# Second attention by whole units of 384 tokens, and a float32 path with TensorE transposes for two batches and two units

## The chip, the cores and the metric

The kernel runs on one core of a Trainium2 chip, written in Bass with the Tile framework. The metric is the time of one execution on the device, in microseconds; lower is better. The core's engines are TensorE (PE in the profile, its weight loads PEld), VectorE (DVE), ScalarE (ACT), GpSimd (POOL) and SyncE (SP). Each runs its own queue of instructions in order. All of this kernel's transfers, transposes by DMA included, are issued from SP's queue.

## The reference

The inputs are q, k, v of shape [8, 8, 576, 64] (batch, head, token, dimension), p of shape [8, 8, 32, 64], and the weights of a gated feed-forward layer, which arrive as 64-bit floats.

```python
def sm_attn(qq, kk, vv):
    s = scale * np.matmul(qq, kk.transpose(0, 1, 3, 2))      # scale = 1/8
    s = s - np.max(s, axis=-1, keepdims=True)
    a = np.exp(s)
    a = a / (np.sum(a, axis=-1, keepdims=True) + 1e-09)
    return np.matmul(a, vv)
p_packed = sm_attn(p, k, v)              # first attention: 32 rows per head
out = sm_attn(q, p_packed, p_packed)     # second attention: 576 tokens over 32 keys
# x: [4608, 512], a token's 8 heads side by side
xn = x / np.sqrt(np.mean(x * x, axis=-1, keepdims=True) + 1e-06) * rms_g
g = xn @ w_gate                          # [512, 1536]
val = xn @ w_val
return (g * (1 / (1 + np.exp(-g))) * val @ w_out)   # w_out [1536, 512]
```

## The kernel before

A product of float32 matrices is made of three f16 matmuls: each operand is scaled and split into a high and a low half (`split`: ACT makes the high half at L127, DVE the low one at L128), and high·high, high·low and low·high are added up in PSUM. Beside f16 there is a float32 path, which needs no split.

The 4608 tokens make 12 units of 384 tokens (`UT`), a unit is 3 tiles of 128 tokens. A batch has 576 tokens, one and a half units, so units 1, 4, 7 and 10 hold tokens of two batches ("mixed" below).

First attention, by batch: `stage1_gen(b)`. It loads the keys (`kf`, L254) and p, takes norms (Square with output `khl`, L390), splits the keys and transposes them by DMA (`kT`, L311), scores `psc` on PE (L331), softmax, transposes of the probabilities on PE (`pat`, L354), values `pp`. Batch 0 instead stays in float32, with keys transposed by TensorE (L295) and scores at L322. Its end result, p_packed, is folded into the gate and value weights: `pw_chunk(b, c)` makes six chunks per batch (`pp_w` on PE at L463, then four ACT and four DVE splits into `pwt`), two of them during the unit ahead and four in the first unit that needs them.

Second attention, by tile of 128 tokens: `qtile_gen(t)` loads q (`qf`, L500), takes its norm and splits it (`qhl`), transposes it by DMA (`qT`, L525), makes the scores `ps` on PE (L550; float32 at L541 for the tiles of unit 0), then max, subtract (L557), exp (ACT, L558), sum, reciprocal and product on DVE, splits the probabilities (`ehl`), transposes them by DMA (`aT`, L574), multiplies by the values (`px`, L581; ACT squares it at L587 for the RMS norm) and POOL makes the norm (`ru`, L594). `unit_gen(u)` then joins the three tiles: a sum over the unit on PE (`pnu`, L609), the scale `rr` by tile, a second split (`ahl`) and a third DMA transpose by tile (`aTu`, L633). Unit 0 has TensorE transposes in place of all three (`pqT` at L505, and `transposed`).

The feed-forward of a unit has two phases. In the first, called gv here, `moe_ft` runs for 12 slices of 128 features: PE makes `pg` and `pv` (L659), ACT applies silu (`t`, L666), DVE multiplies (L667), ACT and DVE split the product into `h` (L669, L670). `pg`, `pv`, `po` and `pp_w` share four PSUM buffers. In the second, called out here, `moe_out` runs 36 matmuls `po` (L680) for each of 3 tiles, DVE scales the result and SP stores it.

The order comes from two places. Python generators are stepped in a written order: a string `PROLOGUE` for the start, then 24 slots per unit, one after each `moe_ft` and one after each group of `po` matmuls; `spread` puts the steps of a generator at slots. The framework's scheduler then orders each engine's queue from that, by its own estimates, and places the semaphores. The step `w` of the prologue is the weight load `weights_gen`, which includes w_out (`wst` loads, conversion to float32, `wo_split` into `wo` at L224 to L229). `big` is a rotating set of buffers (5 in this kernel) for `kf`, `vf`, `khl`, `kT` and the first q.

Where the second attention stands among the slots:

```python
    for t in range(TPU, NU * TPU):
        u, i = divmod(t, TPU)
        at = NS * (u - 1) + 4 * i + 2
        spread(qtile_gen(t), [at - 6, at, at + 3, at + 7, at + 8])
    for u in range(1, NU):
        at = NS * (u - 1) + 19
        spread(unit_gen(u), [at, at + 1, at + 2, at + 3, at + 4])
```

Of the kernel before, what the change touches and what calls it, by code (L numbers as in the profile page):

```python
# [28 lines left out]
def tile_packed_attention_then_swiglu(  # L29
# [41 lines left out]
    HR = H * NPK  # L71
    QK = 1.0 / math.sqrt(D)
# [75 lines left out]
    wctx = ExitStack()  # L148
    wpool = wctx.enter_context(tc.tile_pool(name="wpool", bufs=2))
# [11 lines left out]
    def load_gv(c):  # L161

        pn = ps_m.tile([P, 512], F32, name="pn", tag="pm")
        for n, w in enumerate((w_gate, w_val)):

            room = (2 * c + n) % 5
            if room < 3:
                raw = wo32[:, 4 * room : 4 * room + 4, :].bitcast(U32).rearrange("p a n -> p (a n)")
            else:
                raw = wpool.tile([P, 4 * DM], U32, name="wst", tag="wst", bufs=2)  # L170
# [24 lines left out]
    def load_wo(i):  # L195

        raw = wpool.tile([P, 2, DM, 2], U32, name="wst", tag="wst", bufs=2)
# [4 lines left out]
        to_f32(wo32[:, 2 * i : 2 * i + 2, :], raw)  # L202
        nc.vector.tensor_reduce(
            wo_mx[:, 2 * i : 2 * i + 2], wo32[:, 2 * i : 2 * i + 2, :], AX.X, ALU.max, apply_absolute_value=True
        )

    def wo_scale():

        v = wo_mx.rearrange("p (c f) -> p c f", f=2)
        nc.vector.tensor_mul(v, v, wo_sc.unsqueeze(2).broadcast_to([P, NFC, 2]))  # L210
        mx = wpool.tile([P, 1], F32, name="wmx", tag="w1", bufs=6)
        nc.vector.tensor_reduce(mx, wo_mx, AX.X, ALU.max)
# [18 lines left out]
    def weights_gen():  # L231
        load_g()
        yield
# [3 lines left out]
        for i in range(NFT // 2):  # L237
            load_wo(i)
            yield
        wo_scale()  # L240
        for i in range(NFT // 2):
            wo_split(i)
            yield
# [15 lines left out]
    def stage1_gen(b):  # L259
# [5 lines left out]
        if b == 0:  # L265
# [48 lines left out]
        def scores(g, kT):  # L314
# [3 lines left out]
            if b == 0:  # L318
# [43 lines left out]
        def values(vf, a1T, ri, ss):  # L362

            pp = ps_a.tile([P, 512], F32, name="pp", tag="pa")
            for c in range(NCK):
                for j in range(4):

                    cv = c if b else 2 * (c % HC) + c // HC
# [12 lines left out]
        if b == 0:  # L381
# [41 lines left out]
        if b == 0:  # L423
            first_p.append(pool.tile([P, 4, 2, NPK], F32, name="pbd32", tag="pwt", bufs=8))
            nc.gpsimd.memset(first_p[0], 0.0)
# [6 lines left out]
        for g in range(2):  # L432
            h = slice(64 * g, 64 * g + 64)
            if b == 0:
                nc.vector.tensor_copy(first_p[0][h, :, g, :], pts[h])
            nc.scalar.copy(pbd[h, 0, :, g, :], pts[h])
            nc.vector.tensor_tensor(pbd[h, 1, :, g, :], pts[h], pbd[h, 0, :, g, :], ALU.subtract)
# [36 lines left out]
    first_q = []  # L474
    aTs, e32s, rus, units = {}, {}, {}, {}

    late = []

    def qtile_gen(t):
        u, i = divmod(t, TPU)  # L480

        def mem(name, shape, dt, tag, bufs):

            if t < TPU:
                return pool.tile(shape, dt, name=name, tag="pwt", bufs=8)
            return late[0].tile(shape, dt, name=name, tag=tag, bufs=bufs)

        b0, r0 = divmod(t * P, S)
        parts = [(b0, r0, 0, min(P, S - r0))]
        if r0 + P > S:  # L490
            parts.append((b0 + 1, 0, S - r0, P - (S - r0)))
        if t < TPU:
            if t == 0:
                first_q.append(big([P, TPU, H, D], F32, "q0"))
                nc.sync.dma_start(first_q[0], q[0, :, :UT, :].rearrange("h (s c) d -> s c h d", c=TPU))
            qf = first_q[0][:, t, :, :]
        else:
            qf = mem("qf", [P, H, D], F32, "qf", 2)
# [3 lines left out]
        if t < TPU:  # L502
            ps = ps_m.tile([P, 512], F32, name="pqT", tag="pm")
            for kt in range(NKT):
                nc.tensor.transpose(ps[:, kt * P : (kt + 1) * P], qf[:, 2 * kt : 2 * kt + 2, :].rearrange("s h d -> s (h d)"), ident32)  # L505
            qT = mem("qT32", [P, NKT, P], F32, "", 0)
            nc.vector.tensor_copy(qT.rearrange("p k t -> p (k t)"), ps)
            uq = None
        else:
            uq, qT = split_q(qf, mem)  # L510
        yield
        yield from rest_q(t, u, i, parts, qT, uq, mem)

    def split_q(qf, mem):
        qm = pool.tile([P, 1], F32, name="qm", tag="t1", bufs=14)
        uq = pool.tile([P, 1], F32, name="uq", tag="uq", bufs=6)
        sq = pool.tile([P, 1], F32, name="sq_", tag="t1", bufs=14)
        qhl = mem("qhl", [P, 2, H * D], F16, "qhl", 2)
        nc.scalar.activation(
            qhl[:, 0, :].bitcast(BF16).rearrange("s (h d) -> s h d", h=H), qf, AF.Square, accum_out=qm  # L520
        )
        norm_scale(uq, sq, qm)
        split(*(qhl[:, l, :].rearrange("s (h d) -> s h d", h=H) for l in range(2)), qf, sq)
        qT = mem("qT", [P, 2 * NKT, P], F16, "qT", 2)
        nc.sync.dma_start_transpose(out=qT, in_=qhl.rearrange("s l x -> s (l x)"))  # L525
        return uq, qT

    def rest_q(t, u, i, parts, qT, uq, mem):
        b0 = parts[0][0]
        esc = pool.tile([P, 1], F32, name="esc", tag="uq", bufs=6)  # L530
        eps = packs[b0][1]
        if len(parts) > 1:
            eps = pool.tile([P, 1], F32, name="eps2", tag="eps2", bufs=2)
        ps2 = ps_a.tile([P, H, NPK], F32, name="ps2", tag="pa")
        ps2p = ps2.rearrange("s (e j) r -> s e j r", e=2)
        for b, r, o, n in parts:
            uv, eb, _, pbd, _ = packs[b]
            if uq is None:
                nc.vector.tensor_scalar_mul(esc, uv, 0.5 * QK)
                for pi in range(4):  # L540
                    nc.tensor.matmul(  # L541
                        ps2p[:, :, pi, :], qT[:, pi, :], first_p[0][:, pi, :, :], start=True, stop=True
                    )
                continue
            nc.vector.tensor_scalar(esc[o : o + n], uq[o : o + n], uv[o : o + n], 0.25 * QK, ALU.mult, ALU.mult)
            if len(parts) > 1:
                nc.gpsimd.tensor_copy(eps[o : o + n], eb[o : o + n])
            for pi in range(4):
                for j, (lq, lp) in enumerate(((0, 0), (0, 1), (1, 0))):
                    nc.tensor.matmul(  # L550
                        ps2p[o : o + n, :, pi, :], qT[:, lq * NKT + pi, o : o + n], pbd[:, lp, pi, :, :],
                        start=(j == 0), stop=(j == 2),
                    )
        mx = pool.tile([P, H], F32, name="mx2", tag="t8", bufs=6)
        nc.vector.tensor_reduce(mx, ps2, AX.X, ALU.max)  # L555
        e = pool.tile([P, H, NPK], F32, name="e", tag="e", bufs=4)
        nc.vector.tensor_tensor(e, ps2, mx.unsqueeze(2).broadcast_to([P, H, NPK]), ALU.subtract)  # L557
        nc.scalar.activation(e, e, AF.Exp, scale=esc)  # L558
        sm = pool.tile([P, H], F32, name="sm2", tag="t8", bufs=6)
        nc.vector.tensor_reduce(sm, e, AX.X, ALU.add)  # L560
        ri = pool.tile([P, H], F32, name="ri2", tag="t8", bufs=6)
        nc.vector.tensor_scalar(ri, sm, 1e-9, None, ALU.add)
        nc.vector.reciprocal(ri, ri)
        nc.vector.tensor_tensor(e, e, ri.unsqueeze(2).broadcast_to([P, H, NPK]), ALU.mult)
        ef = e.rearrange("s h r -> s (h r)")
        e32s[t] = ef
        aT = mem("aT", [P, 4, P], F16, "aT", 1)
        if t < TPU:
            transposed(aT[:, :2, :], aT[:, 2:, :], ef, 2.0**14)
        else:  # L570
            ehl = mem("ehl", [P, 2, HR], F16, "ehl", 3)
# [232 lines left out]
```

## Time and profile before

| What | Value |
|---|---|
| runs | 901.73, 900.35, 901.82 us, median 901.73 |
| the profiled execution: its time, its span | 899.14 us, 897.3 us |
| mean granted TensorE clock | 0.949 |
| stages: first `pg` of unit 0, first `po` of unit 0 | 80.2 us, 134.3 us |
| first `pg` of units 1 to 6 | 193.8, 264.8, 326.3, 393.4, 461.4, 524.1 us |
| first `pg` of units 7 to 11 | 592.3, 659.1, 721.6, 787.2, 846.6 us |

The span is the part of an execution that the profiler's engine records cover; the execution's time is 1.84 us more. A unit starts at its first gate matmul. Up to 193.8 us the core loads weights, runs the first attention of batch 0 and unit 0; from there to 846.6 us ten units follow one another, each with the attention of later ones in between; the last unit has nothing beside it. In the profile's groups an "idle before" is idle time of that engine just ahead of the group's instructions, with what ended it.

### The profile page before, as it was taken

The numbers are of one execution on the slowest core, as the hardware profiler recorded it, in microseconds if no ns is written. First come the engines' busy times: TensorE is split into PE (matmuls) and PEld (weight loads), VectorE is DVE, ScalarE is ACT, GpSimd is POOL, SyncE is SP. The second block draws the span as 40 slices with busy tenths as digits, with TensorE's granted clock in tenths as the row PEclk, the third lists the DMA queues.
The fourth block names the chain that finished last, engine by engine and source line by source line (L and its number), as shares of the span: only waits on it lengthen the run. The fifth ranks groups of instructions, "written<-read, shape, count | busy, mean of one in ns | idle before, by whom it ended". The sixth has DMA issues, their size and how long they took to land.

```text
span 897.3 us, 16663 instructions
## 1 busy us (share of the span) xinstructions
PE 762.6 (85%) x6392; PEld 433.7 (48%) x6392; DVE 543.7 (61%) x1397; ACT 554.7 (62%) x1065; POOL 85.9 (10%) x219
## 2 busy tenths in 40 slices
PE   4656758748989898999899889999899899989998
PEld 3432324336645444557455435458455345467453
DVE  3686964636737558467557558368466568466351
ACT  3476676436757569567568479467477578476240
POOL 1243005100000000100010100000000100100000
PEclk8567998959999999999999999999999999999999
DMA  9784263430671472230841652231822712220200
GB/s 246 274 302 139 95 140 75 104 70 7 125 156 30 91 166 54 48 89 7 176 105 31 127 129 54 48 89 31 182 72 60 144 34 56 58 60 19 59 1 36
DMA packets 174000, 84.98 MB, mean 95 GB/s; under 512 B 149216, under 2 KB 161504, under 8 KB 173920
## 3 DMA queue, kind: packets, MB, share of 16 engines
q1 hardware_dynamic: 173920, 83.91, 39.5%
q8 instruction: 50, 0.82, 0.4%
q14 instruction: 30, 0.25, 0.1%
HBM read 47.97 MB, written 9.44 MB: 64 GB/s over the span
## 4 chain that ended last, share of the span: by engine, by line
PE 41%; ACT 20%; DVE 16%; DMA 13%; issue 7%; POOL 2%; SPq 1%; ACTq 0%; DVEq 0%; POOLq 0%
PE po L680 13%; PE pg L659 8%; PE pv L659 8%; DMA aT<-ehl 6%; PE pp_w L463 4%; ACT t L666 3%; ACT L666 3%; PE px L581 2%; DMA kT<-khl 2%; DVE t L667 2%; DMA kf<-in_k_dram 2%; ACT pwt L127 2%; DVE pwt L128 1%; DMA aTu<-ahl 1%; ACT khl L390 1%
## 5 line engine op out<-in xcount | busy, mean ns | idle before, releaser
L680 PE MATMUL po<-wo,h 128*128 128x512 f16 x1296 | 295.1, 382 | 3.8 <-ACT t L666 1.4
L659 PEld LDWEIGHTS <-pwt 128*128 128x128 f16 x2304 | 206.0, 99 | 148.2 <-issue 43.5
L659 PE MATMUL pg<-aTu,pwt 128*128 128x384 f16 (+1 forms) x1152 | 170.6, 289 | 38.7 <-ACT t L666 14.1
L680 PEld LDWEIGHTS <-h 128*128 128x128 f16 x1296 | 123.8, 99 | 156.5 <-issue 20.2
L659 PE MATMUL pv<-aTu,pwt 128*128 128x384 f16 (+1 forms) x1152 | 167.9, 289 | 1.3 <-DVE t L667 0.7
L667 DVE SCALAR_TENSOR_TENSOR t<-pv,usc,t 128x384 f32<-128x384 f32 x144 | 88.3, 614 | 51.6 <-PE pv L659 31.6
L128 DVE SCALAR_TENSOR_TENSOR pwt<-pp_w,pw_sc,pwt 128x256 f16<-128x256 f32 x192 | 84.3, 477 | 53.9 <-ACT pwt L127 52.3
L669 ACT CAST h<-t 128x384 f16<-128x384 f32 x144 | 73.0, 509 | 61.2 <-DVE t L667 60.9
L666 ACT ACTIVATE t<-pg,usc 128x384 f32<-128x384 f32 x144 | 83.0, 578 | 35.6 <-PE pg L659 34.4
L127 ACT ACTIVATE pwt<-pp_w,pw_sc 128x256 f16<-128x256 f32 x192 | 81.5, 470 | 21.7 <-PE pp_w L463 12.2
L670 DVE TENSOR_TENSOR h<-t,h 128x384 f16<-128x384 f32 x144 | 79.8, 555 | 21.5 <-ACT h L669 18.7
L587 ACT ACTIVATE px<-px 128x512 f32<-128x512 f32 x36 | 21.0, 584 | 87.6 <-PE px L581 87.4
L463 PE MATMUL pp_w<-wgv,pg 64*32 64x512 f32 x768 | 57.1, 613 | 2.9 <-ACT t L666 2.1
L685 DVE TENSOR_SCALAR o<-po,invE 128x512 f32<-128x512 f32 x36 | 27.0, 749 | 48.6 <-PE po L680 37.0
L581 PE MATMUL px<-pav,aT 128*128 128x256 f16 (+1 forms) x240 | 32.6, 282 | 23.9 <-DMA aT<-ehl 23.4
L589 POOL TENSOR_SCALAR var<-ssx,eps 128x1 f32<-128x1 f32 x36 | 9.5, 265 | 427.2 <-ACT px L587 427.0
L666 ACT ACT_TABLE_LOAD x35 | 44.9, 1283 | 1.5 <-PE pg L659 0.8
L555 DVE TENSOR_REDUCE mx<-ps 128x8 f32<-128x256 f32 x36 | 15.1, 420 | 40.2 <-PE ps L550 38.3
L581 PEld LDWEIGHTS <-aT 128*128 128x128 f16 (+1 forms) x240 | 20.5, 102 | 38.3 <-DMA aT<-ehl 34.9
L558 ACT ACT_TABLE_LOAD x30 | 38.5, 1283 | 0.5
L128 DVE SCALAR_TENSOR_TENSOR khl<-kf,sk,khl 96x768 f16<-96x768 f32 x28 | 27.7, 1009 | 0.5 <-ACT khl L127 0.5
L560 DVE TENSOR_REDUCE sm<-e 128x8 f32<-128x256 f32 x36 | 15.0, 417 | 19.2 <-ACT e L558 18.9
(260 smaller groups left out, 790.4 us busy)
## 6 DMA issues: line engine op xcount, KB each, us to landing
kf<-in_k_dram SPq DMA_DIRECT2D x16, 576.0 KB, 7.4
vf<-in_v_dram SPq DMA_DIRECT2D x16, 576.0 KB, 6.9
out_dram<-o SPq DMA_DIRECT2D x36, 256.0 KB, 2.2
qf<-in_q_dram SPq DMA_DIRECT2D x29, 256.0 KB, 3.3
wst<-in_moe_w_out_dram SPq DMA_DIRECT2D x6, 1024.0 KB, 5.2
wo<-in_moe_w_gate_dram SPq DMA_DIRECT2D x4, 1024.0 KB, 9.5
wo<-in_moe_w_val_dram SPq DMA_DIRECT2D x4, 1024.0 KB, 7.1
wst<-in_moe_w_val_dram SPq DMA_DIRECT2D x2, 1024.0 KB, 8.1
```

The source lines that it names most:

```text
L127: nc.scalar.activation(hi, x, AF.Copy, scale=s)
L128: nc.vector.scalar_tensor_tensor(lo, x, s, hi, ALU.mult, ALU.subtract)
L463: nc.tensor.matmul(ps[e][32 * j : 32 * j + 32, :], pg[h, j, :], wgv[h, c, j, :, :].rearrange("p w f -> p (w f)"), start=True, stop=True,)
L558: nc.scalar.activation(e, e, AF.Exp, scale=esc)
L581: nc.tensor.matmul(px[o : o + n, 256 * g : 256 * g + 256], aT[:, 2 * la + g, o : o + n], pav[g][:, lp, :], start=(j == 0), stop=(j == 2),)
L659: nc.tensor.matmul(ps[:, c0 : c0 + n], pw[:, g, lw, w, f * P : (f + 1) * P], aT[:, 2 * la + g, c0 : c0 + n], start=(j == 0), stop=(j == 5),)
L666: nc.scalar.activation(t, pss[0], AF.Silu, scale=sc[:, c, 0:1])
L667: nc.vector.scalar_tensor_tensor(t, pss[1], sc[:, c, 1:2], t, ALU.mult, ALU.mult)
L669: nc.scalar.copy(h[:, 0, :], t)
L670: nc.vector.tensor_tensor(h[:, 1, :], t, h[:, 0, :], ALU.subtract)
L680: nc.tensor.matmul(po, hs[ft][:, lh, ts], wo[:, ft, lw, :], start=(n == 0), stop=(n == 3 * NFT - 1))
L685: nc.vector.tensor_scalar_mul(o, po, invE)
```

## The change

1. The generators by tile and by unit become one, `attention_gen(u)`, for all 384 tokens. Partition p of a tile now holds token 3p+i of the unit for tile i, so one load of q brings 768 bytes in a row, and the output rows are stored with the same interleaving. The element-wise steps take all three tiles in one instruction (768 columns), the DMA transposes too: `qT` in 24 blocks, `aT` and `aTu` in 12. In a mixed unit every tile now holds 64 tokens of each batch (`parts`), where before only one of the three tiles was shared.
2. `EARLY = 2`: the float32 path with TensorE transposes is used for the first attention of batches 0 and 1 and for the second attention of units 0 and 1.
3. The steps of a unit's attention stand at the slots `U_AT` of the unit ahead. Batch 1's first attention starts in the prologue, beside unit 0's gv phase.
4. w_out is loaded in 8 pieces through `big` buffers (now 6, also for q, `qhl`, `qT`), and split (`wo_split`) after unit 0's gv phase. `h` of all slices is one tile, `hall`.

The core of the diff:

```diff
-WOS = "ADADDA"
-PROLOGUE = "s w " + "s " * 13 + "0 1 2 " * 5 + "u " * 4 + "w " * 18 + "p a a w " * 6 + "w " * 6
+BIG = 6
+PROLOGUE = "s g " + "s " * 13 + "u " * 6 + "w " * 18 + "p a a S o " * 6 + "o " * 2
+S1_AT = [n for n in range(20)]
+U1_AT = [12, 13, 14, 17, 18, 19, 20]
+U_AT = [-2, 4, 11, 17, 19, 21]
...
+    EARLY = 2
...
+    hall = cpool.tile([P, NFT, 2, UT], F16, name="hall")
...
+    def big(shape, dt, name):
+        return pool.tile(shape, dt, name=name, tag="big", bufs=BIG)
...
+        r, n = divmod(i, 2)
+        raw = big([P, 3, 2 * P, 2], U32, "raw")
         nc.sync.dma_start(
             raw.rearrange("p a n e -> p a (n e)"),
-            w_out[2 * i * P : 2 * (i + 1) * P, :].rearrange("(a p) n -> p a n", p=P),
+            w_out[3 * r * P : 3 * (r + 1) * P, 4 * P * n : 4 * P * (n + 1)].rearrange("(a p) n -> p a n", p=P),
...
+    def wout_gen():
+        for i in range(8):
             load_wo(i)
             yield
         wo_scale()
-        for i in range(NFT // 2):
+        for i in range(NFC):
             wo_split(i)
...
-        if b == 0:
+        early = b < EARLY
+        if early:
...
-    def qtile_gen(t):
...
-            for b, r, o, n in parts:
-                nc.sync.dma_start(qf[o : o + n], q[b, :, r : r + n, :].rearrange("h s d -> s h d"))
...
-        qT = mem("qT", [P, 2 * NKT, P], F16, "qT", 2)
-        nc.sync.dma_start_transpose(out=qT, in_=qhl.rearrange("s l x -> s (l x)"))
...
+    def parts(u):
+
+        b, r = divmod(u * UT, S)
+        n = min(P, (S - r) // TPU)
+        return [(b, r, 0, n)] + ([(b + 1, 0, n, P - n)] if n < P else [])
+
+    def attention_gen(u):
+        early = u < EARLY
+        q_ = big([P, H, TPU, D], F32, "q")
+        for b, r, o, n in parts(u):
+            nc.sync.dma_start(
+                q_[o : o + n].rearrange("s h c d -> s h (c d)"),
+                q[b, :, r : r + TPU * n, :].rearrange("h (s c) d -> s h (c d)", c=TPU),
+            )
+        yield
+            qT = big([P, TPU, NKT, P], F32, "qT32")
+            for i in range(TPU):
+                ps = ps_m.tile([P, 512], F32, name="pqT", tag="pm")
+                for h in range(H):
+                    kt, e = divmod(h, 2)
+                    nc.tensor.matmul(
+                        ps[64 * e : 64 * e + 64, kt * P : (kt + 1) * P], q_[:, h, i, :], ident32, start=True, stop=True
+                    )
+                (nc.vector.tensor_copy if i != 1 else nc.scalar.copy)(qT[:, i].rearrange("p k t -> p (k t)"), ps)
...
+            qhl = big([P, 2, TPU, H * D], F16, "qhl")
...
+            qT = big([P, 2, TPU, NKT, P], F16, "qT")
+            nc.sync.dma_start_transpose(
+                out=qT.rearrange("p l c k t -> p (l c k) t"), in_=qhl.rearrange("s l c x -> s (l c x)")
+            )
...
+        psx = ps_a.tile([P, 2 * 512], F32, name="ps2", tag="psc", bufs=1)[:, : TPU * HR]
...
+        nc.vector.tensor_reduce(mx, psg, AX.X, ALU.max)
+        e = pool.tile([P, TPU, HR], F32, name="e", tag="e", bufs=1)
+        nc.vector.tensor_tensor(eg, psg, mx.unsqueeze(2).broadcast_to([P, NG, NPK]), ALU.subtract)
         nc.scalar.activation(e, e, AF.Exp, scale=esc)
...
+            transposed(aT, e, 2.0**14)
+        else:
...
+            nc.sync.dma_start_transpose(
+                out=aT.rearrange("p i l g t -> p (i l g) t"), in_=ehl.rearrange("s i l x -> s (i l x)")
+            )
+        yield
...
+        for i in range(TPU):
+            px = ps_a.tile([P, 512], F32, name="px", tag="pa")
+            for b, r, o, n in parts(u):
...
+        ru2 = pool.tile([P, TPU], BF16, name="ru2", tag="ru2", bufs=2)
+        nc.gpsimd.tensor_tensor(ru2, ru, ru, ALU.mult)
+        yield
...
+            nc.sync.dma_start_transpose(
+                out=aTu.rearrange("p i l g t -> p (i l g) t"), in_=ahl.rearrange("s i l x -> s (i l x)")
+            )
+        yield
...
-    for t in range(TPU, NU * TPU):
-        u, i = divmod(t, TPU)
-        at = NS * (u - 1) + 4 * i + 2
-        spread(qtile_gen(t), [at - 6, at, at + 3, at + 7, at + 8])
-    for u in range(1, NU):
-        at = NS * (u - 1) + 19
-        spread(unit_gen(u), [at, at + 1, at + 2, at + 3, at + 4])
-    NS1 = 13
-    for b in range(1, B):
-        t = b * S // P
-        u, i = divmod(t, TPU)
-        end = NS * (u - 1) + 4 * i + 2 + 2
-        spread(stage1_gen(b), [end - 2 * (NS1 - j) for j in range(NS1 + 1)])
+            jobs.setdefault(n, []).append(gen)
+
+    spread(steps["o"], [NFT - 1] * 16)
+    spread(steps["S"], S1_AT)
+    spread(steps["U"], U1_AT)
+    for u in range(EARLY, NU):
+        at = NS * (u - 1)
+        spread(attention_gen(u), [at + n for n in U_AT])
+    for b in range(EARLY, B):
+        u = b * S // UT
+        end = NS * (u - 1) + U_AT[2]
+        spread(stage1_gen(b), [end - 2 * (13 - j) for j in range(14)])
```

What stands in the queues, before and after, at three places. On ACT, at the start of unit 4, a mixed one (`qhl`, `ahl`, `pwt` are splits, L666 is the silu of `moe_ft`). Before:

```order
L127 ACTIVATE ahl<-e,rr 128x256 x3
L127 ACTIVATE qhl<-qf,sq__4417 128x512
L519 ACTIVATE qhl,qm<-qf 128x512
L127 ACTIVATE qhl<-qf,sq__4652 128x512
L127 ACTIVATE pwt<-pp_w,pw_sc 128x256 x4
L666 ACT_TABLE_LOAD
L666 ACTIVATE t<-pg,usc 128x384
L669 CAST h<-t 128x384
L666 ACTIVATE t<-pg,usc 128x384
L127 ACTIVATE pwt<-pp_w,pw_sc 128x256 x4
```

After (the silu is L658, the splits L133, the cast into `hall` L660, the Square of batch 4's keys L394):

```order
L133 ACTIVATE ahl<-e,rr 128x256 x3
L133 ACTIVATE qhl<-q,sq__4107 128x512 x3
L133 ACTIVATE pwt<-pp_w,pw_sc 128x256 x4
L658 ACT_TABLE_LOAD
L658 ACTIVATE t<-pg,usc 128x384
L394 ACTIVATE khl,ssk<-kf_0_4295 96x1536
L660 CAST hall<-t 128x384
L658 ACTIVATE t<-pg,usc 128x384
L133 ACTIVATE pwt<-pp_w,pw_sc 128x256 x2
L394 ACTIVATE khl,ssk<-kf_1_4297 96x1536
L133 ACTIVATE pwt<-pp_w,pw_sc 128x256 x2
L660 CAST hall<-t 128x384
```

The Square of the next batch's keys has moved into the gv phase, behind the first silu. On SP, the loads of a later batch's keys, before (among the small transposes of unit 2):

```order
L311 DMA_TRANSPOSE kT<-khl 128x24x96
L254 DMA vf_0_2443<-in_v_dram 96x4x384
L254 DMA vf_1_2445<-in_v_dram 96x4x384
L574 DMA_TRANSPOSE aT<-ehl 128x4x128
L688 DMA out_dram<-o 128x512
L254 DMA kf_0_2949<-in_k_dram 96x4x384
L254 DMA kf_1_2951<-in_k_dram 96x4x384
L688 DMA out_dram<-o 128x512
```

After, at the start of unit 4:

```order
L570 DMA_TRANSPOSE aT<-ehl 128x12x128
L677 DMA out_dram<-o 128x512 x2
L618 DMA_TRANSPOSE aTu<-ahl 128x12x128
L515 DMA_TRANSPOSE qT<-qhl 128x24x128
L257 DMA kf_0_4295<-in_k_dram 96x4x384
L677 DMA out_dram<-o 128x512
L257 DMA kf_1_4297<-in_k_dram 96x4x384
L570 DMA_TRANSPOSE aT<-ehl 128x12x128
```

The key loads now stand behind two large transposes, `aTu` of unit 4 and `qT` of unit 5. On DVE, the softmax of the second attention at the end of a gv phase, before (the first tile of unit 3):

```order
L555 TENSOR_REDUCE mx_2901<-ps_2887 128x8
L557 TENSOR_TENSOR e<-ps_2887,mx_2901 128x256
L670 TENSOR_TENSOR h<-t,h 128x384
L667 SCALAR_TENSOR_TENSOR t<-pv,usc,t 128x384
L560 TENSOR_REDUCE sm_2906<-e 128x8
L670 TENSOR_TENSOR h<-t,h 128x384
L562 TENSOR_SCALAR ri_2908<-sm_2906 128x8
L563 RECIPROCAL ri_2908<-ri_2908 128x8
L564 TENSOR_TENSOR e<-e,ri_2908 128x256
L667 SCALAR_TENSOR_TENSOR t<-pv,usc,t 128x384
L573 SCALAR_TENSOR_TENSOR ehl<-e,ehl 128x256
```

After (the whole of unit 3):

```order
L450 TENSOR_TENSOR pav<-pw,pav 128x256
L552 TENSOR_REDUCE mx_2798<-ps_2760 128x24
L555 TENSOR_TENSOR e<-ps_2760,mx_2798 128x768
L661 TENSOR_TENSOR hall<-t,hall 128x384
L558 TENSOR_REDUCE sm_2803<-e 128x24
L560 TENSOR_SCALAR ri_2805<-sm_2803 128x24
L561 RECIPROCAL ri_2805<-ri_2805 128x24
L562 TENSOR_TENSOR e<-e,ri_2805 128x768
L569 SCALAR_TENSOR_TENSOR ehl<-e,ehl 128x3x256
L675 TENSOR_SCALAR o<-po,invE 128x512
```

Three chains of a tile each, spread among the slices of gv, have become one chain that starts behind the last slices and ends beside the first `po`. On PE the `px` of a unit follow behind 54 matmuls `po`, where before the three tiles' `px` stood at three places of the gv and out phases. Over the whole program the compiled order has 44 loads of ACT's function table where it had 70, and 48 DMA transposes in place of 120.

More of the change, by code (lines that the diff above doesn't have):

```diff
@@ L637, in segs @@
[L637 to L644 removed]
+        if early:
+            for i in range(TPU):
+                nc.scalar.activation(e[:, i], e[:, i], AF.Copy, scale=rr[:, i : i + 1])
+            transposed(aTu, e, 1.0)
+        else:
+            ahl = pool.tile([P, TPU, 2, HR], F16, name="ahl", tag="ehl", bufs=1)
+            for i in range(TPU):
+                split(ahl[:, i, 0, :], ahl[:, i, 1, :], e[:, i], rr[:, i : i + 1])
+            nc.sync.dma_start_transpose(
+                out=aTu.rearrange("p i l g t -> p (i l g) t"), in_=ahl.rearrange("s i l x -> s (i l x)")
+            )
```

325 lines of the change are left out of this document (123 added, 202 removed).

## The prediction

> **What bounds the kernel now.** I read the page's head first, then the busy time by stage, PE's waits in the steady stage, groups by shape, and the DMA queue. The head:
>
> ```profile
> span 897.3 us, 16663 instructions
> PE 762.6 (85%) x6392; PEld 433.7 (48%) x6392; DVE 543.7 (61%) x1397; ACT 554.7 (62%) x1065; POOL 85.9 (10%) x219
> ```
>
> PE is the fullest engine, but an average hides the stages. The next rows are stretches of the span: length, then PE, PEld, DVE, ACT and POOL busy, the granted clock, DMA share and GB/s.
>
> ```profile
> 0.00:80.20 80.20, 41.55 (x311) 28.14 (x312) 47.35 (x121) 41.63 (x65) 23.11 (x52) 0.68 0.83 255
> 80.20:126.40 46.20, 34.27 (x234) 14.87 (x233) 41.71 (x84) 33.85 (x62) 2.67 (x4) 0.96 0.37 98
> 126.40:193.80 67.40, 40.59 (x356) 19.51 (x356) 35.23 (x104) 36.60 (x72) 17.17 (x21) 0.81 0.42 93
> 193.80:846.60 652.80, 599.34 (x5240) 346.67 (x5240) 402.49 (x1062) 430.56 (x845) 42.96 (x142) 0.99 0.37 81
> ```
>
> From 193.8 us on PE is busy 92% of the time, so whatever the change does there is bounded by 652.8 - 599.3 = 53.5 us of idle PE. From 126.4 to 193.8 us PE is busy only 60%. What PE waits for, first the steady stage (waiter, releaser, total us, times, longest), then one row from 126.4 to 193.8 us, then the first gate matmul of unit 1 with its wait in brackets:
>
> ```profile
> PE px L581 <- DMA aT<-ehl: 14.6, 18, 1.8
> PE pg L659 <- ACT t L666: 13.3, 12, 2.0
> PE pg L659 <- DMA aTu<-ahl: 10.9, 7, 6.1
> PE psc L331 <- DMA kT<-khl: 9.5, 6, 2.3
> PE pg L659 <- DVE pwt L128: 3.5, 3, 1.5
> PE pp_w L463 <- ACT t L666: 2.1, 2, 1.0
> PE ps L550 <- DMA qT<-qhl: 1.3, 2, 0.8
> PE px L581 <- DMA aT<-ehl: 8.8, 3, 6.3
> 193.83 0.50 PE L659 MATMUL pg<-aTu,pwt 128*128 128x192 f16 x2 [6.06 <-DMA aTu<-ahl]
> ```
>
> Two kinds stand out: transposes by DMA (14.6 + 10.9 + 9.5 + 1.3 = 36.3 us in the steady stage) and ACT late with silu or its splits (about 19).
>
> **The change, part by part.** A: the start, up to the first gate matmul of unit 1. Unit 1 goes to TensorE transposes, so the 8.8 and the 6.06 us above go, about 14.9; the new chain (PE, PSUM, an ACT and a DVE pass) leaves perhaps 3, so -12. What the float32 path costs PE is read in the groups of the first 80.2 us, where batch 0 and unit 0 already take it:
>
> ```profile
> L295 PE MATMUL pkT<-ident,kf 96*128 96x96 f32 x24 | 4.1, 368 | 0.0
> L322 PE MATMUL psc<-kT,pT 64*32 64x288 f32 x32 | 3.1, 550 | 0.9 <-ACT a1T L358 0.9
> L354 PE MATMUL pat<-ident,a 128*96 128x128 f32 x12 | 3.0, 426 | 5.0 <-ACT a L344 5.0
> L369 PE MATMUL pp<-vf,a1T 96*32 96x64 f32 x96 | 3.0, 314 | 0.9 <-ACT a1T L358 0.9
> L505 PE MATMUL pqT<-ident,q 128*128 128x128 f32 x12 | 3.1, 428 | 0.0
> L541 PE MATMUL ps<-pbd,qT 128*128 128x64 f32 x24 | 4.6, 361 | 0.0
> ```
>
> The q transposes become 8 matmuls per tile, 24 for unit 1 at 3.1/12 = 0.26 us each: +6. The float32 scores of unit 1: 4.6, less some f16 ones, +4. Batch 1's first attention takes 4.1 + 3.1 + 3.0 + 3.0 = 13.2 us of PE and moves beside unit 0's gv phase; its `pat` and `pp`, 6.0, leave the stage behind: -6. Beside the gv phase (80.2 to 126.4) PE has 46.2 - 34.3 = 11.9 us idle, but DVE is busy 41.7 of 46.2 there, so batch 1 shows: between 0 and 13, I take +4, nearer the low end because the idle of PE nearly holds it. Unit 0's own chain has a third of the small POOL and DVE steps: -3. A is -12 + 6 + 4 - 6 + 4 - 3 = -7. Its bounds are +6 (batch 1 uncovered) and -16 (all waits gone, batch 1 hidden).
>
> B: the waits for DMA transposes. Groups by shape:
>
> ```profile
> L555 DVE TENSOR_REDUCE mx<-ps 128x8 f32<-128x256 f32 x36 | 15.1, 420 | 40.2 <-PE ps L550 38.3 <-PE ps L541 1.9
> L339 DVE TENSOR_REDUCE mx<-psc 128x1 f32<-128x576 f32 x16 | 12.0, 752 | 6.2 <-PE psc L331 4.6 <-PE psc L322 1.6
> L558 ACT ACTIVATE e<-e,esc 128x256 f32<-128x256 f32 x36 | 18.3, 508 | 7.4 <-DVE e L557 7.1
> L680 PE MATMUL po<-wo,h 128*128 128x512 f16 x1296 | 295.1, 382 | 3.8 <-ACT t L666 1.4 <-ACT wo L228 1.4 <-POOL wo L229 1.0
> L581 PE MATMUL px<-pav,aT 128*128 128x256 f16 x192 | 28.2, 283 | 21.5 <-DMA aT<-ehl 21.1 <-ACT px L587 0.2
> L581 PE MATMUL px<-pav,aT 128*64 128x256 f16 x48 | 4.4, 277 | 2.3 <-DMA aT<-ehl 2.3
> L659 PE MATMUL pg<-aTu,pwt 128*128 128x384 f16 (+1 forms) x1152 | 170.6, 289 | 38.7 <-ACT t L666 14.1
> aT<-ehl SPq DMA_TRANSPOSE x33, 2.5
> kT<-khl SPq DMA_TRANSPOSE x14, 5.1
> kf<-in_k_dram SPq DMA_DIRECT2D x16, 576.0 KB, 7.4
> L311 SPq DMA_TRANSPOSE kT<-khl x14: 2884/3000/3411, 118.3 to 704.5; - x14
> ```
>
> Between the end of a gv phase and `px` there now stand 54 `po`, 54 x 295.1/1296 = 12.3 us of cover. The chain beside them: a DVE pass over 768 columns by extension from 0.420 us at 256 and 0.752 at 576 is about 0.95; four or five of them with an exp of 1 to 1.5, one ACT split of about 0.95 and small steps give some 7.7 us; a 12-block transpose lands between the 2.5 us of 4 blocks and the 5.1 us of 24, say 3.8: 11.5 in all. It just fits, so px waits shrink from 14.6 to about 3 and do not vanish. qT, issued long ahead, goes from 1.3 to 0. aTu: 10.9 less the 6.06 at unit 1, counted in A, is 4.8, and becomes about 3, since 12 blocks land later than 4. kT: batch 1 no longer takes it, others keep it, 9.5 to about 4. B is -11.6 - 1.3 - 1.8 - 5.5 = -20; bounds -8 (the longer transposes eat half) and -24.
>
> C: loads of ACT's function table. The compiled order has 44 for 70. Their price, then ACT's load in a gv phase with second attention in it (first half of unit 3):
>
> ```profile
> L666 ACT ACT_TABLE_LOAD x35 | 44.9, 1283 | 1.5 <-PE pg L659 0.8
> L558 ACT ACT_TABLE_LOAD x30 | 38.5, 1283 | 0.5
> 326.30:365.30 39.00, 34.13 (x328) 18.51 (x329) 29.53 (x84) 35.98 (x74) 1.73 (x5) 1.00 0.26 52
> 361.59 1.28 ACT L558 ACT_TABLE_LOAD   x1
> 362.88 0.51 ACT L558 ACTIVATE e<-e,esc 128x256 f32<-128x256 f32 x1
> ```
>
> 26 x 1.283 = 33 us leave ACT. Only where ACT is the bound does that reach the end: in this gv phase, 36.0 of 39.0 us busy. PE's waits for ACT are 13.3 + 2.1 + 3.5 = 18.9 in the steady stage, the ceiling. Half of them is taken, rounded down: -8; bounds 0 and -16. The last two rows show the ACTIVATE starting at 362.88, 0.01 us behind the end of its table load.
>
> [...]
>
> D: PE's extra work. In a mixed unit all three tiles are split: 36 px of half width for 12 full and 12 half. Full ones are 28.2/192 = 0.147 us, half ones 4.4/48 = 0.092: 3.31 - 2.87 = +0.44 a unit. The scores gain 24 matmuls of a quarter of px's columns, between 0 and 24 x 0.092 = 2.2, I take a quarter, 0.6. Four mixed units: +4; bounds +1 and +8.
>
> E: a new wait. On SP the key loads for batches 2, 4 and 6 now stand behind `aTu` and the 24-block `qT`, and on ACT the Square of these keys stands behind the first silu of mixed units 1, 4 and 7. Before, ACT waited little for keys:
>
> ```profile
> ACT khl L390 <- DMA kf<-in_k_dram: 3.9, 3, 1.6
> L390 ACT ACTIVATE khl<-kf 96x1536 bf16<-96x1536 f32 x14 | 20.6, 1474 | 5.3 <-DMA kf<-in_k_dram 3.9 <-issue 1.4
> ```
>
> Let T be the first gate matmul, when aTu has landed. A 24-block transpose holds SP 3.0 us (the row of L311), so part of that runs past T; a key load then takes 5 us or more against a median of 7.4. kf is there about T + 6.4. The first silu ends near T + 2.4, so ACT stands some 4 us, then squares for 1.5. PE meanwhile fills four PSUM buffers, two slices of 12 matmuls at 0.148 (the row of L659), 3.6 us, and then idles. I take 4.5 us an event, three events, +13; bounds 0 (the loads land first) and +21 (7.4 us landing, pwt splits held up too).
>
> [...]
>
> The loads of q in pieces of 768 bytes for 256, POOL's fewer instructions and the interleaved output rows I cost at nothing: POOL is busy 43 of 652.8 us, DMA 37%, and q is loaded a unit ahead. The last unit has nothing beside it and does not change.
>
> Sum: -7 - 20 - 8 + 4 + 13 = -18, against the profiled 899.14: 881. The profiled execution stands 2.6 below the median of 901.73, so in terms of that median 884.
>
> **The rivals.** First, E does not happen: the keys land before the first silu has ended (7.4 us is a median, and the transposes ahead of them may be done by T). Then 884 - 13 = 871, and with C at -16 863. For it speaks that ACT waited 3.9 us in all before; against it the order on SP. Second, slower: the start. w_out comes in 8 pieces, through `big` buffers that batch 1's keys hold until PE has transposed them, and SP stands in order behind the first piece that has no buffer.
>
> ```profile
> wst<-in_moe_w_out_dram SPq DMA_DIRECT2D x6, 1024.0 KB, 5.2
> ```
>
> Six of them that land one by one, 6 x 5.2 = 31 us, against a gv phase of 46.2: if they begin only after its first half, the scale of w_out is late, the six splits stand before the first `po`, and PE has lost half of those 31 us, 16; with batch 1's 13.2 us uncovered as well, 9 above the 4 taken, A is +18 in place of -7: 884 + 25 = 909. It decides from A = +12 on. Against it: the loads are spread over all of the gv phase. Third, the whole-unit transposes are just longer waits, B only -8: 896, inside the forecast's own range. No change within 0.2%, about 1.8 us and what a measurement of this kernel can tell: it takes A at +6, B at -8 and E as forecast.
>
> **How the numbers follow.** The forecast's case, 875 to 900, has 0.50; keys in time or ACT's gain larger, 862 to 875, 0.26; within 0.2% of 901.7, 0.06; slower by the start, 0.18. So faster 0.76, same 0.06, slower 0.18. The predicted time is that of the first. The range from 862 to 905 leaves out the far part of the slower case and little below.
>
> **What would show it.** A: the first gate matmul of unit 1 at about 187 us. B: waits of `px` for `aT` near 3 us in all, of `pg` for `aTu` no larger than 5. C: 44 table loads; the first gv phase of unit 3 below 37 us. E: ACT idle before the Square of keys about 4 us in units 1, 4 and 7, and PE idle behind it. The forecast is wrong if the first `po` comes after 150 us, or if ACT's and DVE's 768-wide steps hold up the silus and PE waits for ACT more than 19 us.

## The result, and the profile after

The changed kernel takes 914.87 us (913.7 to 916.66, four runs), 901.12 before: 1.0154 times as long, 95% interval 1.0135 to 1.0174. The forecast, 884 with a range from 862 to 905, was wrong in sign. The page's head, and the two stages up to unit 11 as busy time (length; PE, PEld, DVE, ACT, POOL busy; clock, DMA share, GB/s):

```profile
span 913.3 us, 16290 instructions
PE 784.1 (86%) x6638; PEld 453.1 (50%) x6638; DVE 515.2 (56%) x1126; ACT 501.2 (55%) x937; POOL 63.3 (7%) x124
0.00:187.45 187.45, 129.59 (x1038) 71.02 (x1039) 120.20 (x253) 103.50 (x172) 35.80 (x62) 0.85 0.49 148
187.45:862.61 675.16, 607.59 (x5350) 357.50 (x5348) 377.85 (x845) 385.71 (x741) 27.45 (x62) 0.97 0.36 79
```

187.45 us is the first gate matmul of unit 1, 193.83 before: the start is 6.4 us shorter. The steady stage is 675.2 us against 652.8: 22.3 longer, though ACT's busy time there fell from 430.6 to 385.7 and DVE's from 402.5 to 377.9. PE is busy 8.3 us longer and idle 14.1 us longer (67.6 for 53.5). The last unit is as before. Sum: -6.4 + 22.3 = 16, the difference of the spans. What PE waits for in the steady stage now:

```profile
PE pg L651 <- ACT t L658: 27.7, 10, 4.8
PE pg L651 <- DMA aTu<-ahl: 17.8, 6, 4.2
PE pg L651 <- DVE pwt L134: 5.5, 3, 1.8
PE px L582 <- DMA aT<-ehl: 4.4, 3, 1.9
PE pp_w L465 <- ACT t L658: 4.2, 3, 1.4
PE psc L335 <- DMA kT<-khl: 3.0, 3, 1.2
PE pp L373 <- ACT a1T L362: 2.5, 3, 0.8
PE pv L651 <- DVE t L659: 1.9, 8, 0.3
```

The px waits fell as forecast (14.6 to 4.4). The waits for silu doubled (13.3 to 27.7), those for `aTu` rose from 4.8, without unit 1, to 17.8. Three places account for this. First, the start of unit 4: rows of the timeline of PE, ACT and SP (start, length, engine; in brackets the idle time before, and its releaser):

```profile
392.99 1.15 PE L651 MATMUL pv<-aTu,pwt 128*128 128x192 f16 x12
398.48 2.08 PE L651 MATMUL pg<-aTu,pwt 128*128 128x192 f16 x12 [4.34 <-ACT t L658]
390.08 0.58 ACT L658 ACTIVATE t<-pg,usc 128x384 f32<-128x384 f32 x1 [1.03 <-PE pg L651]
395.98 1.48 ACT L394 ACTIVATE khl<-kf 96x1536 bf16<-96x1536 f32 x1 [5.32 <-DMA out_dram<-o]
397.86 0.57 ACT L658 ACTIVATE t<-pg,usc 128x384 f32<-128x384 f32 x1
384.28 2.40 SPq L618 DMA_TRANSPOSE aTu<-ahl  x1
386.77 3.78 SPq L515 DMA_TRANSPOSE qT<-qhl  x1
390.64 0.54 SPq L257 DMA_DIRECT2D kf<-in_k_dram  x1
```

ACT stands 5.32 us at the Square, between the first silu and the second, until keys issued at 390.64 have landed, 5.3 us later (the releaser named is another transfer of the moment; the Square reads `kf`). PE fills its four PSUM buffers, then idles 4.34 us. This is the forecast's term E. Second, the end of the out phase of unit 1, where `aTu` of unit 2 is made:

```profile
248.73 1.31 ACT L133 ACTIVATE ahl<-e,rr 128x256 f16<-128x256 f32 x3 [3.07 <-POOL rr L608]
248.96 3.09 SPq L315 DMA_TRANSPOSE kT<-khl  x1
252.11 0.69 SPq L257 DMA_DIRECT2D vf<-in_v_dram  x1
252.89 1.40 SPq L618 DMA_TRANSPOSE aTu<-ahl  x1
259.02 1.14 PE L651 MATMUL pg<-aTu,pwt 128*128 128x384 f16 x6 [3.60 <-DMA aTu<-ahl]
```

The split is done near 250.6, but SP is busy with a 24-block key transpose until 252.05 and issues a value load, and only then `aTu`, which lands 6.1 us later. So it is in units 2, 3, 5, 6, 8 and 9: issued right behind a value load, `aTu` lands 5.8 to 6.6 us later. In units 4, 7, 10 and 11, where no value load is near, it needs 3.2 to 4.1. Third, the end of unit 10's gv phase:

```profile
824.35 1.28 ACT L556 ACT_TABLE_LOAD   x1
825.65 0.94 ACT L556 ACTIVATE e<-e,esc 128x768 f32<-128x768 f32 x1
827.73 1.28 ACT L658 ACT_TABLE_LOAD   x1
829.65 1.21 PE L651 MATMUL pg<-aTu,pwt 128*128 128x192 f16 x12 [3.03 <-ACT t L658]
```

The exp for the whole of unit 11 stands between two table loads among the silus, and PE idles 3.03 us; the same in units 1, 4 and 7. A fourth effect shows in the first fence: 12 matmuls take 2.08 us behind the wait, where the granted clock is 0.50 for 4 us, and 1.15 ahead of it.

### The profile page after: what moved, and what is told of

Same layout as the page of the kernel before. It is cut to its first block, busy times and chain, and to the rows that moved or that the text cites. A ratio compares the mean times of both kernels' runs of the same rounds, so it can differ in the third digit from the quotient of the medians.

```text
span 913.3 us, 16290 instructions
## 1 busy us (share of the span) xinstructions
PE 784.1 (86%) x6638; PEld 453.1 (50%) x6638; DVE 515.2 (56%) x1126; ACT 501.2 (55%) x937; POOL 63.3 (7%) x124
## 5 line engine op out<-in xcount | busy, mean ns | idle before, releaser
L670 PE MATMUL po<-wo,hall 128*128 128x512 f16 x1296 | 293.7, 383 | 6.0 <-POOL wo L237 4.0
L651 PEld LDWEIGHTS <-pwt 128*128 128x128 f16 x2304 | 212.3, 101 | 173.0 <-issue 75.2
L651 PE MATMUL pg<-aTu,pwt 128*128 128x384 f16 (+1 forms) x1152 | 177.1, 299 | 56.9 <-ACT t L658 27.7
L670 PEld LDWEIGHTS <-hall 128*128 128x128 f16 x1296 | 125.0, 99 | 161.8 <-issue 23.1
L651 PE MATMUL pv<-aTu,pwt 128*128 128x384 f16 (+1 forms) x1152 | 172.0, 294 | 2.6 <-DVE t L659 1.9
L658 ACT ACTIVATE t<-pg,usc 128x384 f32<-128x384 f32 x144 | 82.8, 578 | 58.4 <-PE pg L651 57.5
L660 ACT CAST hall<-t 128x384 f16<-128x384 f32 x144 | 73.2, 509 | 73.6 <-DVE t L659 73.4
L661 DVE TENSOR_TENSOR hall<-t,hall 128x384 f16<-128x384 f32 x144 | 79.6, 555 | 50.6 <-ACT hall L660 48.2
L133 ACT ACTIVATE pwt<-pp_w,pw_sc 128x256 f16<-128x256 f32 x192 | 81.4, 470 | 24.2 <-DVE pwt L134 12.4
L394 ACT ACTIVATE khl<-kf 96x1536 bf16<-96x1536 f32 x12 | 17.8, 1481 | 18.2 <-DMA kf<-in_k_dram 12.9
L134 DVE SCALAR_TENSOR_TENSOR khl<-kf,sk,khl 96x768 f16<-96x768 f32 x24 | 23.0, 1010 | 6.1 <-ACT khl L133 6.1
L133 ACT ACTIVATE ahl<-e,rr 128x256 f16<-128x256 f32 x30 | 13.1, 497 | 23.1 <-POOL rr L608 23.1
```

The costliest lines, as they stand in the source:

```text
L133: nc.scalar.activation(hi, x, AF.Copy, scale=s)
L134: nc.vector.scalar_tensor_tensor(lo, x, s, hi, ALU.mult, ALU.subtract)
L651: nc.tensor.matmul(psi[:, :, o : o + n], pw[:, g, lw, w, f * P : (f + 1) * P], aT[:, :, la, g, o : o + n], start=(j == 0), stop=(j == 5),)
L658: nc.scalar.activation(t, pss[0], AF.Silu, scale=sc[:, c, 0:1])
L660: nc.scalar.copy(hall[:, ft, 0, :], t)
L661: nc.vector.tensor_tensor(hall[:, ft, 1, :], t, hall[:, ft, 0, :], ALU.subtract)
```

## The experiments

All are edits of the changed kernel, one of them on top of another. They ran on several chips, so each is given as a ratio to the kernel before, timed on the same chip, with its 95% interval; the changed kernel's is 1.0154. Differences between runs are taken from these ratios.

**Keys earlier.** The key loads of batches 2 to 7 get a generator of their own:

```diff
+    def kload_gen(b):
+        kfd[b] = [load_half(k, "kf", b, g) for g in range(2)]
+        yield
...
+        spread(kload_gen(b), [end - 26 - 8])
         spread(stage1_gen(b), [end - 2 * (13 - j) for j in range(14)])
```

> The changed kernel with the key loads of batches 2 to 7 stepped 8 slots earlier, as a generator of their own, and nothing else; in the queues they then stand ahead of aTu and of the next qT, and the Squares ahead of the first silu. Theory 1 (ACT stands at the Square because the key loads were issued behind two large transposes): PE's three waits for the first silus of units 1, 4 and 7 (3.49 + 4.34 + 4.85 = 12.7 us) go, and with them the half-speed clock that follows each (some 1.9 us apiece): 914.9 - 12.7 - 5.7 = 897, between 894 and 901. Rival (the Squares themselves, two of 1.5 us per batch, are too much for ACT in these phases, wherever the keys are): the wait stays at about 3 us a unit, 908 to 915.

905.32 us, 1.0059 (1.0036 to 1.0082). The gv phases of units 1, 4 and 7 shrank from 39.9, 42.1 and 41.5 us to 35.2, 35.2 and 35.1, 18 us as theory 1 says, and the waits at the first silus are gone. Part is given back: waits for `aTu`, 17.8, are now 21.0, and outside these three phases PE is busy 7 us longer, most of it at a lowered clock behind such waits (the gv phases of units 3 and 9, at a granted clock of 0.94 and 0.93 where it had been 1.00, are busy 5.1 us longer). So the total falls by some 9 only, less than was expected.

```profile
PE pg L659 <- DMA aTu<-ahl: 21.0, 6, 4.1
PE pg L659 <- ACT t L666: 15.0, 7, 3.0
```

**aTu in three.**

```diff
                 split(ahl[:, i, 0, :], ahl[:, i, 1, :], e[:, i], rr[:, i : i + 1])
-            nc.sync.dma_start_transpose(
-                out=aTu.rearrange("p i l g t -> p (i l g) t"), in_=ahl.rearrange("s i l x -> s (i l x)")
-            )
+                nc.sync.dma_start_transpose(
+                    out=aTu[:, i].rearrange("p l g t -> p (l g) t"), in_=ahl[:, i].rearrange("s l x -> s (l x)")
+                )
```

> The changed kernel with the last transpose, aTu, issued as three of 4 blocks, each behind its tile's split, in place of one of 12. Theory A (the transpose of 12 blocks simply lands later: 5.8 us in the median against 2.5 for 4 blocks before): PE's waits for aTu, 17.8 us over units 2, 3, 5, 6, 8 and 9, fall below 8 and the time to about 905. Theory B (aTu stands on SP behind kT transposes and behind the value loads, and its landing is late because these share the DMA engines): waits stay above 13, time 911 to 917, since SP still holds all three behind the same instructions.

911.33 us, 1.0137 (1.0095 to 1.0179). Waits for `aTu` are 13.0, at the edge of what theory B said, and the total does not differ clearly. The 4.8 us that go would fit six times 0.8, by which 12 blocks with no value load near land later than 4 (3.2 us and, in the median, 2.4). Size is the smaller part.

**Last steps earlier.**

```diff
-U_AT = [-2, 4, 11, 17, 19, 21]
+U_AT = [-2, 4, 11, 17, 18, 20]
```

> The changed kernel with the two last steps of a unit's attention one slot earlier (slots 18 and 20 for 19 and 21); in SP's queue aTu of units 2, 5 and 8 then stands ahead of both value loads, that of units 3, 6, 9 still behind one. Theory B (position behind the value loads): the waits of units 2, 5 and 8 (3.60 + 4.18 + 3.31 = 11.1 us) fall to about 1 us each, those of units 3, 6, 9 (6.7 us) by at most half: 914.9 - 8 to 11, some 905. Theory A (length of the transpose): each wait falls by at most the 0.7 us or so of half a slot, 911 to 914.

902.2 us, 1.0023 (1.0002 to 1.0045). Units 2, 5 and 8 no longer wait for `aTu`; there it stands ahead of both value loads and lands in 3.3 us. In units 3, 6 and 9 the step is one slot earlier too, but `aTu` still stands behind a value load: it lands in 5.8 to 6.1 us, and PE waits 2.59, 2.03 and 2.08, 6.7 in all as before. So it is the position on SP, with 12 blocks in one transpose, and not the earlier step by itself. Theory B holds, and gains a little more than was expected.

```profile
PE pg L651 <- DMA aTu<-ahl: 6.7, 3, 2.6
```

The median time from issue to landing, in the changed kernel, with three transposes of 4 blocks, and with the steps earlier:

```profile
aTu<-ahl SPq DMA_TRANSPOSE x10, 5.8
aTu<-ahl SPq DMA_TRANSPOSE x30, 2.4
aTu<-ahl SPq DMA_TRANSPOSE x10, 3.3
```

**No exp.** `AF.Copy` for `AF.Exp` in the second attention, which leaves out the exponential and, with it, 14 table loads.

> The changed kernel with Copy in place of Exp in the second attention, so that ACT loads 30 function tables for 44 (the output is not the softmax's). Theory C (the whole unit's exp, 0.94 us between two table loads of 1.28, stops the silus for longer than PE's four PSUM buffers hold, once in each of units 1, 4, 7 and 10, 3.03 us each, and each stop ends in half-speed clock): these four waits go, -12, and some 1.9 us of clock each, -7: about 896. Rival (ACT is short of time all over the gv phase, table loads are not what PE waits for): 14 loads of 1.28 less give below 5 us, 910 or more.

903.71 us, 1.0047 (1.0028 to 1.0065): some 10 us faster than the changed kernel, between theory C (19) and its rival (below 5). The four waits of 3.03 us are gone, as theory C says, and waits for silu fall from 27.7 to 18.3; but waits for `aTu` rise to 19.8, and `pg` and `pv` still take 286.7 us of PE, 290.6 in the changed kernel. It leaves open whether the loads or their place matter, so the next run moves the exp.

**Exp behind the silus.**

```diff
+        if u % 3 == 2:
+            nc.vector.scalar_tensor_tensor(esc, hall[:, NFT - 1, 1, 0:1], 0.0, esc, ALU.mult, ALU.add)
         nc.scalar.activation(e, e, AF.Exp, scale=esc)
```

> The changed kernel, but in units 1, 4, 7 and 10 the exp of the next unit's attention may start only behind the last slice of the gv phase (one small DVE step that adds zero times that slice to its scale). All 44 table loads stay. Theory C (what PE waits for is the place of the exp among the silus): the four waits of 3.03 us go and some half-speed clock with them, gv of unit 10 falls from 35.2 to about 31, the time by 12 to 18, to 897 to 903; what could come back is a wait of px for aT, up to 1.5 us in each of four units. Rival (it is the number of table loads that costs): no gain, 912 or more.

904.19 us, 1.0065 (1.0035 to 1.0095), some 8 us faster than the changed kernel, about as much as without exp, and less than expected. The four waits are gone (waits for silu 14.1 for 27.7), but waits for `aTu` grew to 19.2, and `pv` waits 4.3 us for DVE where it waited 1.9. The px waits stay at 4.2.

Not all 44 table loads stay: the trace has 38. In units 1, 4 and 7 the moved exp comes into the out phase, where the exp of a first attention follows: the two share one load of their table, and two loads per unit go. Unit 10 has no such first attention and keeps both of its loads:

```profile
825.50 1.28 ACT L558 ACT_TABLE_LOAD   x1
845.07 1.28 ACT L660 ACT_TABLE_LOAD   x1
```

Its gv phase, which ends at 824.05 here, falls from 35.2 to 31.1 us. So in unit 10 what PE paid for is the place and not the number of loads; in the other three units the run does not separate the two causes.

What a load took can be read in unit 10 of the changed kernel: a silu ends at 824.33, the load runs from 824.35 to 825.63 and the exp starts at 825.65, 1.32 us from one to the other.

**Two together.** The first and third edits.

> Key loads 8 slots earlier and the last two steps one slot earlier, together. Each alone brought about 10 and 12.5 us; alone, the early keys left waits for aTu of 21.0 us, and the earlier steps left the waits at the Squares. If the two places are independent the gains add and more: steady stage 675 - 18 (gv of units 1, 4, 7) - 15, about 645, the time about 885, faster than before by 1.5%. If they fight over SP (keys and aTu in the same stretch of its queue), less than the sum: 895 or more.

873.46 us, 0.9717 (0.9691 to 0.9743): more than the sum of the two, which would be some 20 us, against 39. In SP's queue `aTu` now comes ahead of both value loads in every unit, lands in 3.2 to 4.1 us, and its waits fall to 0.5 us. Gone from the steady stage are 12.7 us of waits for the first silus, 17.3 for `aTu` and 8.7 us of `pg` and `pv` (290.6 to 281.9); new are waits of 6.2 us for `ru`:

```profile
PE pg L659 <- ACT t L666: 15.0, 7, 3.0
PE pnu L604 <- POOL ru L600: 6.2, 7, 1.1
PE pg L659 <- DVE pwt L134: 5.5, 3, 1.8
```

**All three.**

> Key loads 8 slots earlier, last two steps one slot earlier, exp behind the last silus in units 1, 4, 7, 10. By the three theories together: about 885 less 12 to 16, 869 to 875, faster than before by some 3%. Rival (the waits are replaced by others, of px for aT or at the start of units): 880 or more.

858.63 us, 0.9542 (0.952 to 0.9564), 4.6% faster than the kernel before, below every forecast. The trace again has 38 table loads. The steady stage, its matmuls `pg` and `pv`, and the longest waits (the last three rows):

```profile
184.53:805.39 620.86, 591.81 (x5349) 346.22 (x5348) 377.68 (x851) 376.17 (x733) 31.11 (x62) 1.00 0.38 84
L661 PE MATMUL pg<-aTu,pwt 128*128 128x192 f16 (+1 forms) x1008 | 137.9, 281 | 9.3 <-DVE pwt L134 5.5 <-ACT t L668 2.9 <-DMA aTu<-ahl 0.8
L661 PE MATMUL pv<-aTu,pwt 128*128 128x192 f16 (+1 forms) x1008 | 137.3, 280 | 4.5 <-DVE t L669 3.9
PE pnu L606 <- POOL ru L602: 6.1, 7, 1.0
PE pg L661 <- DVE pwt L134: 5.5, 3, 1.8
PE pp_w L473 <- ACT t L668: 4.2, 3, 1.4
```

PE is idle 29.1 us there, and busy 591.8, less than the 607.6 of the changed kernel for the same matmuls. In the changed kernel `pg` and `pv` had taken 147.1 + 143.5 = 290.6, here 275.2. The granted clock is 1.00 here in every gv phase of the stage, where the changed kernel had 0.88 to 0.96 in units 1, 4, 5, 6, 7 and 10: so the 15.4 us are the clock. The two rows of the changed kernel:

```profile
L651 PE MATMUL pg<-aTu,pwt 128*128 128x192 f16 (+1 forms) x1009 | 147.1, 293 | 51.0 <-ACT t L658 27.7 <-DMA aTu<-ahl 17.8 <-DVE pwt L134 5.5
L651 PE MATMUL pv<-aTu,pwt 128*128 128x192 f16 (+1 forms) x1008 | 143.5, 289 | 2.0 <-DVE t L659 1.9
```

**One early.** `EARLY = 1`, at the same slots.

> The changed kernel with the float32 path and TensorE transposes for batch 0 and unit 0 alone; batch 1 and unit 1 by halves and DMA transposes, at the same slots. By the prediction's term A (unit 1 and batch 1 in float32 save about 7 us of the start): first gate matmul of unit 1 at 193 to 197 us instead of 187.5, the time 920 to 925. Rival (the start got shorter only because w_out and the units were moved, not by the path): first gate matmul within 2 us of 187.5, time 913 to 917.

933.43 us, 1.0368 (1.0316 to 1.042). The first gate matmul of unit 1 comes at 202.2 us, 14.7 later than with two: the float32 path does shorten the start, by twice what was expected. Another 5.7 us are lost in the steady stage, which was not foreseen.

**PE kept busy.** To the kernel with early keys, 14 idle-filling matmuls ahead of the units that waited for `aTu`:

```diff
+        for _ in range(14):
+            nc.tensor.matmul(pd[:, :UT], ident, hall[:, NFT - 1, 0, :], start=True, stop=True)
...
+        if u > 1 and u % 3 != 1 and u < NU - 1:
+            warm()
```

> The kernel with early key loads (905.3 us, a ratio of 1.0059 to the kernel before), with 14 matmuls of 384 columns by an identity, whose product nobody reads, put on PE between the last po and the first gate matmul of units 2, 3, 5, 6, 8 and 9, where PE waited 2.8 to 4.2 us for aTu. aTu itself comes no earlier. Theory H (an idle PE of some 3 us is granted half the clock for the next 3 to 4 us): the idle left is 0.6 to 2 us, the granted clock behind the waits stays near 1, pg and pv need some 282 us of PE instead of 291.7, and the time falls by 7 to 10, to 895 to 898, though PE does 13 us more of work. Rival (the half clock follows the heavy DMA traffic of the value loads, or a fixed beat): the clock behind the waits is as before, time 903 to 908.

894.56 us, 0.9938 (0.9917 to 0.9959), 1.2% faster than the same kernel without them, with 14.6 us of PE work more; `pg` and `pv` take 283.6 us for 291.7. The first 4 us behind the wait, in units 3, 5 and 9, without the added matmuls and then with them; the seventh group of numbers is the clock:

```profile
318.57:322.57 4.00, 4.00 (x19) 1.69 (x23) 0.00 (x0) 0.58 (x1) 0.00 (x0) 0.50 1.10 210
455.08:459.08 4.00, 4.00 (x13) 1.92 (x13) 0.00 (x0) 0.58 (x1) 0.00 (x0) 0.50 1.09 272
720.40:724.40 4.00, 4.00 (x19) 1.69 (x22) 0.00 (x0) 0.58 (x1) 0.00 (x0) 0.50 1.10 210
```

```profile
319.38:323.38 4.00, 4.00 (x34) 1.87 (x35) 1.19 (x3) 1.70 (x4) 0.00 (x0) 1.00 1.10 210
453.46:457.46 4.00, 4.00 (x26) 2.26 (x25) 0.62 (x1) 1.46 (x3) 0.00 (x0) 1.00 1.10 273
716.63:720.63 4.00, 4.00 (x34) 1.87 (x35) 1.19 (x3) 1.69 (x4) 0.00 (x0) 1.00 1.10 210
```

Same DMA share, twice the matmuls in the second set. In units 2 and 6 the clock of these 4 us was 0.67 and 0.57 without the added matmuls and is 1.00 with them; in unit 8 it was 1.00 in both. The half clock follows PE's idleness, not the transfers. Theory H holds, except that not every such idle is followed by it.

## Why the prediction was wrong

| term | forecast | measured |
|---|---|---|
| A, the start | -7 | -6.4 |
| B, waits for DMA transposes, steady | -20 | -5.0 (30.2 to 25.2) |
| C, waits for ACT and DVE, without E | -8 | about +7 (22 to 29) |
| D, PE's extra work | +4 | +8.3 of busy time, of it `pg` and `pv` +11.0 |
| E, Square of late keys | +13 | +12.7 (3.49 + 4.34 + 4.85) |

A's total and E were right, E in place, mechanism and size; so were px (-10.2 for -11.6), kT (-6.5 for -5.5) and qT. Inside A the parts were off, and that they came to the right sum is luck: the run with one early batch shows 14.7 us gained from the float32 path, so the rest of the new start costs about 8. The sum is known to some 3 us only, as the first gate matmul of unit 1 came between 183.2 and 188.1 us in the seven runs whose edits begin behind it (187.45 in the changed kernel).

B failed at the step "becomes about 3, since 12 blocks land later than 4": `aTu` went to 17.8. It was priced by its own length. Its length was the smaller matter: with no value load near, its 12 blocks land in 3.2 us (4.1 in unit 4), where 4 took 2.5. What counts is what stands just ahead of it on SP: behind a load of values (576 KB) it lands in 5.8 to 6.6 us. The run that only moved two steps by one slot, in the three units where that changed the order, and the two edits together show this: they leave its 12 blocks whole, the key transposes still stand ahead of it, and the wait is gone. The forecast had read SP's order for the keys (E) but not for `aTu` itself.

C failed at "Half of them is taken": fewer loads were taken to mean less waiting. The gv phase of unit 3, the one where ACT was busy 36.0 of 39.0 us, went only to 38.0 although ACT's busy time in it (the fifth number) fell to 28.6:

```profile
322.28:360.32 38.04, 34.80 (x406) 19.21 (x407) 27.71 (x71) 28.63 (x63) 0.90 (x2) 1.00 0.40 85
```

So it was not ACT's sum that bounded it; the 3.2 us in which PE is idle there are two waits, 1.82 for `pwt` and 1.42 for a silu. The ceiling itself was misread: of the 18.9 us, 3.5 had DVE as their releaser. The silus wait behind single long stops, and one exp for 384 tokens, with a split and a cast before the next table load, made a longer one (3.03 us) than the exp of one tile had in the kernel before (1.98 in each of units 1, 4, 7 and 10). Moving the exp gave what leaving it out gave, within the intervals.

D failed in kind. Its extra px and scores cost nothing that can be seen (px and ps together 43.4 us before, 41.8 after). What grew is `pg` and `pv`, 279.6 to 290.6, and that is the clock behind long idles: before, it was 0.94 and 0.95 in the gv phases of units 1 and 4 and 1.00 in the others of the stage; after, 0.88 to 0.96 in six of them. Their rows before:

```profile
L659 PE MATMUL pg<-aTu,pwt 128*128 128x192 f16 (+1 forms) x1008 | 140.4, 283 | 28.1 <-ACT t L666 13.3 <-DMA aTu<-ahl 10.9 <-DVE pwt L128 3.5
L659 PE MATMUL pv<-aTu,pwt 128*128 128x192 f16 (+1 forms) x1008 | 139.2, 283 | 1.3 <-DVE t L667 0.7
```

The sum counted each idle once, and a stop of 3 to 5 us cost some 2 us more: with the keys early the three phases gained 18 us for 12.7 us of idle. This term was missing from the forecast.

The slower rival was the wrong one: the start as a whole got shorter. The first `po` of unit 0 came at 138.3 us for 134.3, and PE's waits for the split of w_out grew only from 2.4 to 6.0 us. The rival of no change was not added up rightly: A at +6 and B at -8 make 884 + 13 + 12 = 909. Of the two signs listed for a wrong forecast, one appeared: PE waits for ACT well over 19 us (27.7 at `pg`, of which 12.7 are E, and 4.2 at `pp_w`).

The three combined edits leave the work of the change as it is, but for six table loads, and move its transfers and its exp: their places made it slow. What part of the 41 us between the combined version and the kernel before comes from whole units and what from the better places cannot be told, since the edits were not tried in the kernel before.

## What to carry to other kernels

Merging small steps into large ones went here with less busy time (ACT 385.7 us for 430.6 in the steady stage), but each large piece was one longer stop on its queue (an exp of 0.94 us for 0.51): ask for every merged instruction what stands behind it (silus behind an exp), and for every merged transfer what stands ahead of it (value loads ahead of a transpose). Count stops by their length against the buffers that cover them, not by their sum. Where an experiment removes one of several waits, the others can grow until the last is gone: here some 9, 12 and 8 us alone made 55 together.

## What the hardware showed that was not expected

In the steady stage of the changed kernel PE idles twelve times for 2.27 to 4.85 us ahead of a gate matmul. Behind nine of these idles the granted clock was 0.50 for 2.9 to 5.5 us, in two of the nine (3.03 us each, in units 4 and 10) only from some 1 us behind the idle on; behind the other three (3.60, 3.31 and 2.27 us) it stayed at 1.00. In the kernel with early keys the clock of the next 4 us was 0.50 to 0.67 in units 2, 3, 5, 6 and 9, behind waits of 3.73, 3.73, 4.15, 2.92 and 2.84 us, but 1.00 in unit 8 behind 3.65. In the kernel before it fell behind one of the four waits of 1.98 us alone (unit 4: a mean clock of 0.57 in the 4 us from 406.64, 1.00 behind the other three). So the length of an idle does not by itself tell whether the half speed follows, and what else does, no run shows. In the steady stage of the changed kernel the half clock cost 15.4 us of 913.3, 1.7%: `pg` and `pv` take 290.6 there, and 275.2 with all three edits, where no wait is longer than 1.82 us and the clock is 1.00.
